# Code layout, output transfers and the order of the last sums in a decode kernel (attention over a KV cache, then a gated MLP)

**Chip, cores, metric.** One core of one Trainium2 chip. The metric is the device time of one execution in microseconds (us), the median of several executions on one chip. The record marks all runs told here as fast. Engines: PE is TensorE, DVE VectorE, ACT ScalarE, POOL GpSimd, SP SyncE. Times within an execution count from the start of its profiled span.

## The reference

For two sequences with one new token each, layer norm, 32 heads of attention over 8192 cached keys and values of 128 numbers, an output projection, then a second layer norm and a gated MLP, both with residuals:

```python
q = (x @ wq).reshape(B, Sq, Hq, Dh).transpose(0, 2, 1, 3)            # B=2, Sq=1, D=512, Hq=32, Dh=128
scores = einsum("bhqd,bhkd->bhqk", q, k_cache) * Dh ** -0.5           # k_cache, v_cache: (2, 32, 8192, 128) bf16
o = einsum("bhqk,bhkd->bhqd", softmax(scores), v_cache)
h = x + o.transpose(0, 2, 1, 3).reshape(B, Sq, Hq * Dh) @ wo
gate, up = layernorm(h) @ W_gate, layernorm(h) @ W_up                 # F = 1376
out = h + ((gate * (gate > 0)) * up) @ W_down
```

The two caches are 268 MB of the 281 MB that are read.

## The kernel before

All instructions are written to one list for each engine, with the semaphore waits worked out from what is read and written. Heads go in 16 steps of four; a step holds 8.39 MB of K and as much of V. DVE multiplies a K tile by the query in place and halves it to 8 columns; ACT takes the exponentials and their sums (`zm`); PE multiplies by V in a hardware loop; DVE picks the lanes. After the last step:

```python
s.op("pool", lambda: pool.tensor_tensor(out=zl, in0=zl, in1=zx, op=ALU.add),    # last exponential sums
     reads=["zm", "zx"], writes=["zm"], extra=[v_done(L)])
...                              # issue of gate, up0, up1, wda, wdb, wdc, wdd (the MLP's weights) on SP
s.op("pe", lambda: pe.matmul(out=zb, lhsT=same..., rhs=zm..., start=True, stop=True),
     reads=["zm", "same"], writes=["sm"])
lanes(L)
gather(B * NGR - 1)
s.op("dve", ... zs = zb * head_blk); red(zi, zs, ...); s.op("dve", ... zi = 1 / zi)
for k in range(NGR):
    s.op("dve", ... oc[k] = ou[:, :, k] * zi)
...                              # projection by wo, second layer norm, gate products
s.op("pe", lambda: y_rows(eye_of[:, 0:B], ar, first=True), ...)                 # residual into y
s.op("pe", lambda: mlp_in(1, up_ps, 0, KC - 1), reads=["hd", "up0"], writes=["mm1"])
s.op("pe", lambda: mlp_in(1, up_ps, KC - 1, KC), reads=["hd", "up1"], writes=["mm1"])
...                              # gate * up, its columns by PE, copied by ACT and DVE
for key, act_key, f0, f1 in (("wda", "act_t", 0, FT), ("wdb", "act_t", FT, FA),
                             ("wdc", "act_l", FA, FC - 1), ("wdd", "act_l", FC - 1, FC)):
    if key == "wdd":
        for eng in ("pe", "dve", "act"):
            s.cut(eng)                                                           # the late block begins
    s.op("pe", lambda f0=f0, f1=f1: add_y(f0, f1), reads=[act_key, key], writes=["y"])
y0, y1 = slice(0, B), slice(2 * Q, 2 * Q + B)          # partitions 0-1: left half of y, 64-65: right half
s.op("dve", lambda: dve.tensor_copy(y_row[y0], y_ps[y0]), reads=["y"], writes=["y0"])
s.op("act", lambda: act.activation(out=y_row[y1], in_=y_ps[y1], func=ACT.Copy), reads=["y"], writes=["y1"])
for b, eng, e in ((0, "sp", sync), (1, "act", act)):
    ends.append(s.dma(eng, f"dy{b}", lambda b=b, e=e: e.dma_start(
        out=out[b].rearrange("s (c n) -> (s c) n", n=D // 2),
        in_=y_row[b:P:2 * Q]), reads=["y0", "y1"]))    # partitions b and b + 64
```

Each of PE, ACT and DVE has its program in a main block, a late block with the end, and an unused block of `SPARE` empty instructions (15 for ACT, 1 for DVE, 7 for PE). At the start of the first two the program emits a branch hint for the branch at their end (BRANCH_PREFETCH_HINT in the trace: 0.04 to 0.06 us each, at 0.98 to 1.36 us and at 652.01 to 654.01 us).

The softmax here doesn't subtract the row's maximum and nothing guards it: scores larger than these inputs give would overflow.

Of the kernel before, what the change touches and what calls it, by code (L numbers as in the profile page):

```python
# [104 lines left out]
def kernel(  # L105
# [20 lines left out]
    G = 4  # L126
# [29 lines left out]
    RING = T * Dh  # L156
    SPARE = {"act": 15, "dve": 1, "pe": 7}

# [62 lines left out]
    s = Streams(nc, ("pe", "dve", "act", "pool", "sp"))  # L221
    for name in ("v_in", "v_two", "p_in", "p_two", "o_in", "half", "q0", "q1"):
        s.sem(name)
# [5 lines left out]
    for name, value in (("v_two", 16 * (NLOOP - 1)), ("p_two", NLOOP), ("o_in", 1), ("q0", 1),  # L229
                        ("q1", 1)):  # L230
        s.lists["pool"].append(((), lambda name=name, value=value: pool.sem_inc(s.sem(name), value),
                                None))
# [80 lines left out]
    def columns_of_x():  # L313
        for c in range(KC):
# [11 lines left out]
        reads=["xc", "st"], writes=["xd"])  # L326
    s.op("dve", lambda: dve.tensor_tensor(out=sq, in0=xd, in1=xd, op=ALU.mult), reads=["xd"],
         writes=["sq"])
# [5 lines left out]
    s.op("dve", lambda: dve.reciprocal(out=rstd, in_=rstd), reads=["rstd"], writes=["rstd"])  # L334
    s.op("dve", lambda: dve.tensor_tensor(
        out=xnb, in0=_view(xd, 0, [[B, KC], [1, B], [0, Q]]),
# [43 lines left out]

    def products(n, lo, hi, early=()):
        b, i = divmod(n, NQ)
        kp = kt[n % 2][:, lo:hi, :]
        keys = [f"k{n % 2}{x}" for x in parts(lo, hi)] or [f"k{n % 2}b", f"k{n % 2}c"]
        qk = [f"q{b}{i % 2}{h}" for h in range(G)]
        s.op("dve", lambda: dve.tensor_tensor(  # L386
            out=kp, in0=kp, in1=_view(qrep[:, b, i, :], 0, [[0, hi - lo], [1, Dh]]),
            op=ALU.mult), reads=keys + qk, writes=keys)
        width = Dh
        while width > 8:  # L390
            half = width // 2
            s.op("dve", lambda half=half, width=width: dve.tensor_tensor(  # L392
                out=kp[:, :, 0:half], in0=kp[:, :, 0:half], in1=kp[:, :, half:width], op=ALU.add),
                reads=keys + list(early), writes=keys)
            width = half
# [32 lines left out]
    def v_loop():  # L428
        base["pe"] = s.count["pe"]
        s.wait("pe", [s.last[k] for k in ("spread", "pm")])  # L430

        def take(name, value):
            pe.wait_ge(s.sem(name), value).then_inc(s.sem(name), -value)  # L433

        def fn():
            with pe.Fori(0, NGR * B):
                with pe.Fori(0, NS):
                    take("v_in", 16)
                    take("p_in", 1)
                    take("o_in", 1)  # L440
                    v_matmuls(0, T // 2).then_inc(s.sem("half"), 1)
                    take("v_two", 16)
                    v_matmuls(T // 2, LATE)
                    take("p_two", 1)
                    v_matmuls(LATE, T).then_inc(s.sem("pe"), 1)
                pe.wait_ge(s.sem("o_in"), 1)
                for u in range(NS):
                    last = pe.matmul(out=rep_ps[u * Q:(u + 1) * Q, :],  # L448
                                     lhsT=spread.rearrange("k h m -> k (h m)"), rhs=osb[:, u, :],
                                     start=True, stop=True, skip_group_check=True)  # L450
                last.then_inc(s.sem("pe"), 1)

        s.lists["pe"].append(((), fn, None))
        s.count["pe"] += NGR * B * (NS + 1)
# [24 lines left out]

    HALVES = (0, T // 2, T)  # L480
    load_v(0)
    v_loop()
    for n in range(N):
        b, i = divmod(n, NQ)
        z = zm[:, b, i:i + 1]
        for lo, hi in zip(HALVES[:-1], HALVES[1:]) if n == 0 else ((0, T if n < L else LATE),):
            products(n, lo, hi, [f"q{b}{i}{G - 1}" for b in range(B) for i in range(2)] if lo else ())
        if n:
            lanes(n - 1)
            s.last["pm"] = v_done(n - 1)  # L490
        if n % NS == 1 and n > 1:
# [21 lines left out]
    for k, lo, hi in WO:  # L513
# [17 lines left out]
    s.op("pool", lambda: pool.tensor_tensor(out=zl, in0=zl, in1=zx, op=ALU.add),  # L531
         reads=["zm", "zx"], writes=["zm"], extra=[v_done(L)])

# [16 lines left out]
    def load_down(key, f0, r0, rows, r):  # L550
# [9 lines left out]

    s.op("pe", lambda: pe.matmul(out=zb, lhsT=same.rearrange("p u h m -> p (u h m)"),
                                 rhs=zm.rearrange("p b i -> p (b i)"), start=True, stop=True),
         reads=["zm", "same"], writes=["sm"])
    lanes(L)
    gather(B * NGR - 1)
    s.op("dve", lambda: dve.tensor_tensor(
        out=zs, in0=zb.rearrange("p (g u) -> p g u", u=NS),
        in1=_view(head_blk, 0, [[0, B * NGR], [1, NS]]), op=ALU.mult), reads=["sm", "head"],
        writes=["zs"])
    red(zi, zs, AXIS.X, ["zs"], ["zi"])  # L570
    s.op("dve", lambda: dve.reciprocal(out=zi, in_=zi), reads=["zi"], writes=["zi"])
    for k in range(NGR):
        s.op("dve", lambda k=k: dve.tensor_tensor(
            out=oc[:, k * JG:(k + 1) * JG, :], in0=ou[:, :, k].rearrange("p b j -> p j b"),
            in1=_view(zi, k, [[0, JG], [NGR, B]]), op=ALU.mult),
            reads=[f"ou{b * NGR + k}" for b in range(B)] + ["zi"], writes=[f"oc{k}"])
# [65 lines left out]
    def mlp_in(g, ps, c0, c1):  # L642
        for c in range(c0, c1):
            for j in range(FT):
# [14 lines left out]
        out=gt, in0=gate_ps[:, 0:NM], scalar1=0.0, scalar2=r2, op0=ALU.max, op1=ALU.mult),  # L659
        reads=["gate_o", "r2"], writes=["osb0", "osb1", "osb2", "osb3"])  # L660
    s.op("pe", lambda: y_rows(eye_of[:, 0:B], ar, first=True), reads=["eye", "om"], writes=["y"])
    s.op("pe", lambda: mlp_in(1, up_ps, 0, KC - 1), reads=["hd", "up0"], writes=["mm1"])
    s.op("pe", lambda: mlp_in(1, up_ps, KC - 1, KC), reads=["hd", "up1"], writes=["mm1"])
    s.op("dve", lambda: dve.tensor_tensor(
        out=gn.rearrange("p (q j) -> p q j", j=FT), in0=_view(gt, 2 * P, [[1, NQR], [0, FT]]),
        in1=_view(head_blk, 0, [[0, NQR], [1, FT]]), op=ALU.mult),
        reads=["osb0", "head"], writes=["gn"])
    s.op("dve", lambda: dve.tensor_tensor(out=actr, in0=gt[:, 0:2 * P], in1=up_ps[:, 0:2 * P],
                                          op=ALU.mult), reads=["osb0", "mm1"], writes=["act"])
# [15 lines left out]
    def columns_of_rest():  # L685
        for u in range(3):
# [5 lines left out]
    s.op("pe", columns_of_act, reads=["act", "ident"], writes=["sm"])  # L692
    s.op("pe", columns_of_rest, reads=["act_n", "row_b"], writes=["rep"])
    s.op("act", lambda: act.activation(out=act_t[:, 0:FA], in_=act_ps, func=ACT.Copy),
         reads=["sm"], writes=["act_t"])
# [7 lines left out]
    for key, act_key, f0, f1 in (("wda", "act_t", 0, FT), ("wdb", "act_t", FT, FA),  # L703
                                 ("wdc", "act_l", FA, FC - 1), ("wdd", "act_l", FC - 1, FC)):
        if key == "wdd":
            for eng in ("pe", "dve", "act"):
                s.cut(eng)
        s.op("pe", lambda f0=f0, f1=f1: add_y(f0, f1), reads=[act_key, key], writes=["y"])
# [5 lines left out]
    ends = []  # L714
    for b, eng, e in ((0, "sp", sync), (1, "act", act)):
        ends.append(s.dma(eng, f"dy{b}", lambda b=b, e=e: e.dma_start(
            out=out[b].rearrange("s (c n) -> (s c) n", n=D // 2),
            in_=y_row[b:P:2 * Q]), reads=["y0", "y1"]))
    sems = [h.num for h in s.sems.values()]
# [8 lines left out]

    engines = (("sp", sync), ("pool", pool), ("act", act), ("dve", dve), ("pe", pe))
    inner = nc.cur_bb  # L730
    for name, engine in engines:
        only = OrderedEngineSet([engine.engine])
        if name in s.cuts:
            nc.br(f"{name}_all", engines=only)
        else:
            s.emit(name, engine)
            nc.br("done", engines=only)
    for name, engine in engines[2:]:
        only = OrderedEngineSet([engine.engine])
        nc.switch_body(f"{name}_all", parent=inner, valid_engines=only)  # L740
        top = nc.cur_bb
        turn = nc.alloc_registers(f"{name}_turn", engines=only)
        nc.regs_mov(turn, 0)
        loc = engine.mark_branch_hint_location()
        s.emit(name, engine, 0, s.cuts[name])
        engine.br_lt(turn, 9, on_true=f"{name}_late", on_false=f"{name}_spare").branch_hint(loc)
        nc.switch_body(f"{name}_late", parent=top, valid_engines=only)
        loc = engine.mark_branch_hint_location()
        s.emit(name, engine, s.cuts[name])
        engine.br_lt(turn, 9, on_true="done", on_false=f"{name}_spare").branch_hint(loc)  # L750
        nc.switch_body(f"{name}_spare", parent=top, valid_engines=only)
        for _ in range(SPARE[name]):
            engine.nop("spare")
        nc.br("done", engines=only)
    nc.switch_bb("done", parent=inner)
# [28 lines left out]
```

## Time and profile before

| | kernel before |
|---|---|
| time, median | 659.8 us (659.77 to 659.95, 3 runs) |
| span of the profiled run | 657.9 us |
| read from HBM | 281.06 MB |
| DVE busy | 613.6 us, 93% |
| DMA queue of the data (q1) busy | 99.0% |

The prediction below shows the slices, the queues and the chain. The DMA queues of the kernel before in the stretch from 640 to 646 us (packets, MB, share of the sixteen engines' time):

```profile
q1 hardware_dynamic: 292, 2.49, 99.4%
q8 instruction: 1, 0.02, 1.1%
```

One of 293 packets is no data but code (kind "instruction", 16384 bytes, 1.06 us at 642.40), brought in while the last weights are on their way. And the end of the instructions in order of time (start, duration, engine, line, operation, count, and in brackets what ended the idle time before):

```profile
654.42 0.38 ACT L712 ACTIVATE sc<-y 2x256 bf16<-2x256 f32 x1 [2.32 <-PE y L635]
654.42 0.41 DVE L711 CAST sc<-y 2x256 bf16<-2x256 f32 x1 [1.89 <-PE y L635]
654.88 0.62 SPq L716 DMA_DIRECT2D out_dram<-sc  x1
654.88 0.61 ACTq L716 DMA_DIRECT2D out_dram<-sc  x1
```

Both halves of the result are copied at once, and both output transfers take 0.6 us to issue, twice what SP needs for a K tile of 8.39 MB (0.33 us).

### The profile page before, as it was taken

The page shows a single profiled execution, that of the slowest core. Times are in us where ns is not written, and L with a number is a line of the kernel's source. Part 1 is how long each engine was busy: PE and PEld are TensorE (multiplying, and loading weights), DVE is VectorE, ACT ScalarE, POOL GpSimd, SP SyncE. Part 2 cuts the span into 40 slices and gives each one's busy share as a digit, 9 for nine tenths or more (in the row PEclk, how much of TensorE's full clock was granted, in tenths as well). Part 3 has the DMA queues.
Part 4 walks back from the last instruction along what each step waited for, and adds up shares of the span by engine and source line. Part 5 has one row for each costly group of instructions (what it writes and reads, how often), then busy time and mean ns, then how long its engine had stood idle before and what let it go on. Part 6 is the DMA issues. An engine that isn't in the chain of part 4 may idle for free.

```text
span 657.9 us, 3103 instructions
## 1 busy us (share of the span) xinstructions
PE 121.5 (18%) x1206; PEld 49.6 (8%) x1206; DVE 613.6 (93%) x177; ACT 61.9 (9%) x160; POOL 5.6 (1%) x25
## 2 busy tenths in 40 slices
PE   2400302003030110303012030300203030031256
PEld 1100101001010000101000010100101010010022
DVE  1699999999999999999999999999999999999963
ACT  2501001010101001010100101010010101001010
POOL 2000000000000000000000000000000000000000
PEclk9855755657555565755556575555657555565657
DMA  9999999999999999999999999999999999999996
GB/s 379 450 446 426 402 446 446 446 419 410 446 446 438 430 406 446 446 438 430 406 446 446 438 430 406 446 446 438 430 406 446 446 438 430 406 446 415 442 412 267
DMA packets 6614, 281.13 MB, mean 427 GB/s; under 512 B 744, under 2 KB 848, under 8 KB 1360
## 3 DMA queue, kind: packets, MB, share of 16 engines
q1 hardware_dynamic: 6596, 281.06, 99.0%
q8 instruction: 2, 0.03, 0.0%
q14 instruction: 4, 0.03, 0.0%
q10 hardware_dynamic: 12, 0.01, 0.0%
HBM read 281.06 MB, written 0.00 MB: 427 GB/s over the span
## 4 chain that ended last, share of the span: by engine, by line
DVE 75%; DMA 24%; issue 0%; SPq 0%; PE 0%
DVE k L386 34%; DVE k L392 33%; DMA k<-in_A_k_cache_dram 21%; DVE sc L243 4%; DMA k<-in_B_W_down_dram 3%; DVE osb L468 2%; DVE om L463 1%; SPq L539 0%; PE y L635 0%; DVE ou L243 0%; DVE rep L475 0%; SPq L551 0%; DVE sc L711 0%; SPq L294 0%; SPq L779 0%
## 5 line engine op out<-in xcount | busy, mean ns | idle before, releaser
L386 DVE TENSOR_TENSOR k<-k,qrep 128x32768 bf16<-128x32768 bf16 (+3 forms) x18 | 275.8, 15323 | 5.9 <-DMA k<-in_A_k_cache_dram 5.9
L392 DVE TENSOR_TENSOR k<-k 128x4096 bf16<-128x4096 bf16 (+6 forms) x72 | 267.4, 3714 | 2.5
L418 PE MATMUL o<-v,pm 128*32 128x512 bf16 x1024 | 96.3, 556 | 477.6 <-PEq L433 477.6
L405 ACT ACTIVATE pm<-sc 32x256 bf16<-32x256 f32 (+2 forms) x68 | 48.0, 706 | 560.3 <-DVE sc L243 559.6
L418 PEld LDWEIGHTS o<-v,pm 128*32 128x32 bf16 x1024 | 39.1, 132 | 534.3 <-issue 529.5
L243 DVE TENSOR_REDUCE sc<-k 128x256 f32<-128x2048 bf16 (+2 forms) x17 | 36.6, 2152 | 0.1
L468 DVE TENSOR_REDUCE osb<-om 128x128 f32<-128x512 f32 x16 | 16.3, 1018 | 0.6
L405 ACT ACTIVATION_READ_ACCUMULATOR pm<-sc 32x1 f32 x68 | 15.7, 232 | 0.0
L463 DVE TENSOR_TENSOR om<-o,turn_of 128x512 f32<-128x512 f32 x16 | 10.9, 683 | 3.7 <-PE o L418 3.7
L350 PE MATMUL mm<-v,om 128*64 x32 | 9.6, 436 | 7.1 <-PEq L348 7.0
L243 DVE TENSOR_REDUCE pick<-ident 128x8 f32<-128x128 bf16 x1 | 0.4, 381 | 10.9 <-ACT qrep L367 10.9
L367 ACT ACTIVATE qrep<-mm 32x512 bf16<-32x512 f32 x16 | 9.4, 587 | 6.7 <-PE mm L350 6.5
L448 PE MATMUL rep<-osb,spread 128*32 128x128 f32 x32 | 2.6, 421 | 37.9 <-DVE osb L468 37.9
L320 DVE COPY xc<-st 128x8 f32<-128x8 f32 x1 | 0.2, 167 | 6.0 <-PE st L315 6.0
L531 POOL TENSOR_TENSOR zm<-zm,zx 128x1 f32<-128x1 f32 x1 | 0.2, 190 | 626.5 <-PE o L418 626.5
L350 PEld LDWEIGHTS mm<-v,om 128*64 128x64 bf16 x32 | 3.9, 122 | 12.4 <-issue 11.6
L601 DVE STREAM_TRANSPOSE osb<-mm 128x512 f32<-128x512 f32 x1 | 0.7, 717 | 4.1 <-PE mm L587 4.1
L448 PEld LDWEIGHTS rep<-osb,spread 128*32 128x32 f32 x32 | 0.8, 142 | 40.3 <-DVE osb L468 40.3
L587 PE MATMUL mm<-k 128*2 128x512 bf16 x32 | 3.6, 624 | 0.0
L711 DVE CAST sc<-y 2x256 bf16<-2x256 f32 x1 | 0.4, 411 | 1.9 <-PE y L635 1.9
L475 DVE TENSOR_TENSOR rep<-rep,pick 128x128 f32<-128x128 f32 x4 | 1.2, 293 | 0.8 <-PE rep L448 0.8
L635 PE MATMUL y<-k 128*2 128x256 bf16 x22 | 1.8, 271 | 0.4 <-DMA k<-in_B_W_down_dram 0.3
(80 smaller groups left out, 32.2 us busy)
## 6 DMA issues: line engine op xcount, KB each, us to landing
v<-in_A_v_cache_dram SPq DMA_DIRECT2D x4, 4096.0 KB, 20.3
k<-in_A_k_cache_dram SPq DMA_DIRECT2D x2, 4096.0 KB, 26.1
v<-in_A_wq_dram SPq DMA_DIRECT2D x1, 4096.0 KB, 12.3
k<-in_A_wo_dram SPq DMA_DIRECT2D x1, 2048.0 KB, 20.2
k<-in_A_wo_dram SPq DMA_DIRECT2D x2, 1024.0 KB, 23.2
k<-in_B_W_gate_dram SPq DMA_DIRECT2D x1, 1376.0 KB, 13.7
k<-in_B_W_up_dram SPq DMA_DIRECT2D x1, 1032.0 KB, 15.8
k<-in_B_W_down_dram SPq DMA_DIRECT2D x2, 512.0 KB, 17.6
```

What stands on the lines that cost most here:

```text
L243: s.op("dve", lambda: dve.tensor_reduce(out=out_, in_=in_, axis=axis, op=ALU.add), reads=reads, writes=writes)
L350: last = pe.matmul(out=mm_ps[t][0:B * Q], lhsT=xnb[:, c].rearrange("p b q -> p (b q)"), rhs=wq_r[:, c, :, bass.ds(r * 2 + t, 1), :], start ...
L367: fn = lambda src=src, dst=dst: act.activation(out=dst, in_=src, func=ACT.Copy)
L386: s.op("dve", lambda: dve.tensor_tensor(out=kp, in0=kp, in1=_view(qrep[:, b, i, :], 0, [[0, hi - lo], [1, Dh]]), op=ALU.mult), reads=keys ...
L392: s.op("dve", lambda half=half, width=width: dve.tensor_tensor(out=kp[:, :, 0:half], in0=kp[:, :, 0:half], in1=kp[:, :, half:width], op=AL ...
L405: last = act.activation(out=p_of[ps, lo // TG:hi // TG, :, h], in_=sc2[n % 2][ps, lo:hi].rearrange("p (g t) -> p g t", t=TG), func=ACT.Exp ...
L418: last = pe.matmul(out=o_ps[g:g + W2], lhsT=pm[:, t // TG, :], rhs=vt[:, t:t + TG, :].rearrange("p t d -> p (t d)"), start=(t < P // Q * T ...
L448: last = pe.matmul(out=rep_ps[u * Q:(u + 1) * Q, :], lhsT=spread.rearrange("k h m -> k (h m)"), rhs=osb[:, u, :], start=True, stop=True, s ...
L463: s.op("dve", lambda: dve.tensor_tensor(out=om.rearrange("p (t d) -> p t d", d=Dh), in0=o_ps.rearrange("p (t d) -> p t d", d=Dh), in1=_vie ...
L468: s.op("dve", lambda: dve.tensor_reduce(out=osb[:, n % NS, :], in_=om.rearrange("p (t d) -> p d t", d=Dh), axis=AXIS.X, op=ALU.add), reads ...
L587: last = pe.matmul(out=ar_ps[g:g + B], lhsT=oc[:, k, :], rhs=wo_sb[:, k, :], start=False, stop=(k + P // Q >= NK), skip_group_check=True)
L635: end = pe.matmul(out=y_ps[c * 2 * Q:c * 2 * Q + m], lhsT=lhsT, rhs=rhs[:, c * D // 2:(c + 1) * D // 2], start=first, stop=last, skip_grou ...
```

## The change

Its intent: keep instruction fetches out of the time in which the last weights land, take work off the end, and let each output transfer wait for one copy only. The core of the diff (cut):

```diff
-    SPARE = {"act": 15, "dve": 1, "pe": 7}
+    MIDDLE = {"act": 30, "dve": 100, "pe": 9}
@@ first layer norm: two small operations from dve to pool
-    s.op("dve", lambda: dve.tensor_tensor(out=sq, in0=xd, in1=xd, op=ALU.mult), reads=["xd"],
+    s.op("pool", lambda: pool.tensor_tensor(out=sq, in0=xd, in1=xd, op=ALU.mult), reads=["xd"],
@@ V loop: the z product moves in, once for each group of four steps
+                take("z_in", 1)
+                pe.matmul(out=zb, lhsT=same..., rhs=zm..., start=True, stop=True).then_inc(s.sem("z_out"), 1)
@@ first tile: both halves halved once, the rest over the whole tile
+            products(n, 0, T // 2, to=Dh // 2)
+            products(n, T // 2, T, to=Dh // 2)
+            products(n, 0, T, Dh // 2, early=...)
@@ after the last step
     lanes(L)
-    gather(B * NGR - 1)
...
     for k in range(NGR):
+        if k == NGR - 1:
+            gather(B * NGR - 1)
@@ residual rows behind up, and the cut there
+    s.wait("pe", [s.last["up1"]])
     s.op("pe", lambda: mlp_in(1, up_ps, KC - 1, KC), reads=["hd", "up1"], writes=["mm1"])
+    s.cut("pe")
+    s.op("pe", lambda: y_rows(eye_of[:, 0:B], ar, first=True), reads=["eye", "om"], writes=["y"])
...
+    s.wait("dve", [up_mostly]); s.cut("dve")
...
+    s.wait("act", [s.last["up1"]]); s.cut("act")
@@ output
-    for b, eng, e in ((0, "sp", sync), (1, "act", act)):
-            out=out[b].rearrange("s (c n) -> (s c) n", n=D // 2),
-            in_=y_row[b:P:2 * Q]), reads=["y0", "y1"]))
+    for c, rows, eng, e in ((0, y0, "sp", sync), (1, y1, "act", act)):
+            out=out.rearrange("b s d -> (b s) d")[:, c * D // 2:(c + 1) * D // 2],
+            in_=y_row[rows]), reads=[f"y{c}"]))
@@ layout of pe, act and dve: gate, all, last, rest
+        block("gate"); fork(1, "last", False, "all")          # turn 0: on to "all"; turn 1: to "last"
+        block("all");  loc = engine.mark_branch_hint_location()
+        s.emit(name, engine, 0, MIDDLE[name]); fork(1, "rest", True, "last")
+        block("last"); s.emit(name, engine, s.cuts[name]);     fork(1, "done", False, "rest")
+        block("rest"); s.emit(name, engine, MIDDLE[name], s.cuts[name])
+        nc.regs_mov(turn, 1)
+        fork(9, "gate", True, "done").branch_hint(loc)         # back to the first block, then "last"
```

## The prediction

> **What bounds the kernel now.** I read the page first (busy shares, slices, queues), then the chain that ended last, then busy time by stretch, and the order of instructions over the last 25 us. DVE is busy 613.6 of 657.9 us, so it looks like the bound, but the slices say that it isn't alone:

> ```profile
> DVE  1699999999999999999999999999999999999963
> DMA  9999999999999999999999999999999999999996
> GB/s 379 450 446 426 402 446 446 446 419 410 446 446 438 430 406 446 446 438 430 406 446 446 438 430 406 446 446 438 430 406 446 446 438 430 406 446 415 442 412 267
> q1 hardware_dynamic: 6596, 281.06, 99.0%
> q8 instruction: 2, 0.03, 0.0%
> q14 instruction: 4, 0.03, 0.0%
> ```

> The DMA row is full from the first slice to the last but one. A KV step moves 2 x 8.39 MB, which at 446 GB/s is 37.6 us; a DVE step is 17.14 + 8.70 + 4.43 + 2.30 + 1.22 + 0.61 + 1.02 + 2.19 = 37.6 us from the chain. The two are level, and the chain decides:

> ```profile
> 22.94 8.70 DVE k L386
> ...
> 477.38 39.51 DMA k<-in_A_k_cache_dram
> 516.91 17.24 DVE k L386
> ...
> 555.32 38.98 DMA k<-in_A_k_cache_dram
> 594.32 12.97 DVE k L386
> ...
> 635.01 18.08 DMA k<-in_B_W_down_dram
> 653.09 0.04 issue
> 653.13 0.60 PE y L635 x8
> ...
> 654.42 0.41 DVE sc L711
> ```

> Up to 400 us the chain is all DVE; then it jumps three times onto a K load: DVE has caught up and waits for K. The end hangs on W_down. I also counted, from the DMA packet records of the trace, how many are in flight: 15 or 16 or more at every moment from 2.5 us to about 651.5 us (times from the span's start). The transfers form one unbroken run, and nothing before it can end earlier unless that run does. Busy time by stretch shows where it ends:

> ```profile
> 648.00:651.00 3.00, 3.00 (x30) 1.13 (x22) 1.42 (x4) 0.00 (x0) 0.00 (x0) 0.54 1.03 407
> 651.00:654.00 3.00, 1.89 (x27) 0.90 (x25) 1.02 (x3) 0.18 (x1) 0.00 (x0) 0.90 0.39 139
> ```

> The last two columns (DMA share, GB/s) fall from 1.03 to 0.39: the transfers run out in this stretch, but not together. In the packet records most of the sixteen engines finish their part of W_down between 651.6 and 652.5 us, one at 652.91 and one at 653.41 us. The laggards have a visible reason. Queue q8, kind "instruction", put one 16384-byte packet of 1.06 us on an engine at 642.40 us, when PE was at the start of the attention projection; q14 put two 8192-byte packets (0.33 and 0.31 us) in at 138.1 and 140.7 us. 653.41 - 1.06 = 652.35 and 652.91 - 0.63 = 652.28: the laggards are late by just these packets, since no engine has a pause in which to catch up. PE's last products sit right behind them:

> ```profile
> 649.45 1.69 PE L645 MATMUL mm<-k,sc 128*32 128x344 bf16 x16
> 653.13 0.31 PEld L635 LDWEIGHTS y<-k 128*2 128x2 bf16 x8 [0.56 <-DMA k<-in_B_W_down_dram]
> 654.10 0.09 PEld L635 LDWEIGHTS y<-k 128*2 128x2 bf16 x2 [0.19 <-DMA k<-in_B_W_down_dram]
> ```

> So the time is: the unbroken DMA run, plus the lag of its latest engine (about 0.9 us), plus 654.10 to 657.9 us for the last two products, two copies, the output and the closing barrier.

> [...]

> **The change part by part.**

> Start: two small operations of the layer norm go from DVE to POOL (0.17 and 0.42 us on DVE; perhaps 0.3 us slower by POOL with its waits, an estimate from the 0.2 to 0.3 us of its casts here). They end near 9.5 us, and the query projection waits for wq until 13.8 us. Worth 0.

> First tile: the two halves are halved once each, and the other three additions run over the whole tile. Before: 2 x (2.30 + 1.24 + 0.70) = 8.48 us; after: 4.43 + 2.30 + 1.22 = 7.95 us. With three gaps of 0.02, DVE gains 0.6 us at 57 us. DVE waits for K later (0.86 us at 594 us), so this only lengthens that wait. On the end: 0.

> z sums inside the V loop, gather behind: before, after the last lane sums (638.7 us) DVE did gather (0.30 + 0.29), zs 0.16, sum 0.17, reciprocal 0.18, product 0.15, and PE began its projection at 640.87 us. After, the z product runs while DVE does the lane sums, so zs to the first product (about 0.8 us with gaps) follow at once and PE starts near 639.6 us. Gain about 1.2 us there, if the output weights are down. The gate products started at 647.04 us, when gate landed anyway (its last packet ended at 646.43, and completions are seen some 0.5 us after). Alone worth 0; but it lets the weights, if they land 0.9 us sooner, be used sooner.

> Residual rows behind up: 0.5 us of PE moves from 648.92, where PE waited for up, to the wait for DVE's products (651.13 to 651.67). Neutral.

> Code layout: this is the part that can move the end. Each of PE, ACT and DVE gets a first block with the hint, a last part in the middle of the next block, and a rest behind it; after the rest it jumps back to the first block and on to the last part. [...]the packets at 642.4 and at 138 to 141 us go, or come only at the re-entry, after up has landed. Then the latest engine ends at about 652.5 (the next one in the list) instead of 653.41: -0.9 us for W_down and about -0.8 for gate and up. Also the branch and hint between the W_down parts (653.83 to 654.10 us on PE) go: -0.1, as they partly lie beside the landing. Against it: PE's, ACT's and DVE's two taken branches[...] (the ones here record 0.07 to 0.31 us), during waits for up, and a new ACT table load of 1.28 us. With up1 seen at about 649.5, ACT is through it at 651.2; its copy is due at 651.0. The W_down products need 1.3 us of PE, so they would be done at 652.8 if their data were there: still behind the landing. Costs 0.

> Output by tile: each output DMA waits for its own copy only; both copies end within 0.04 us (654.80, 654.83). -0.05 on ACT's issue at most.

> Sum: -0.9 - 0.1 - 0.05, of which I take back 0.25 because the fetches may return near the end on some engine: -0.8 us. 659.8 - 0.8 = 659.0 us.

> **Rivals.**

> (1) The re-entry misses: the block must be fetched at about 650.5 us, while the queues are full; a packet of 1.06 us plus about 1 us from issue to first packet (as SP's first load shows: issued 0.96, first packet 2.0) stalls PE, ACT or DVE by some 2 us. PE would be ready at 653.5 instead of 652.2 and end its products near 655: +0.6, 660.4 us.[...]

> (2) The fetches don't go but move: any fetch before the last W_down packet costs its engine the same 1 us. Then the landing stays and only 0.1 us is gained: 659.7 us.

> (3) DVE becomes the bound: no, DVE's work shrinks by 0.6 us and it already waits for K.

> (4) The exit gets quicker or slower beyond the span: three fetches start at 656.5 to 657.0 us, the longest ending at 657.8, as the span ends. The time is 1.9 us over the span, and if some of that is the exit's code, having it earlier may give another 0.5 us: 658.5.

> **Range and chances.** Two per cent is 13.2 us. The unbroken run of transfers is the same 281.06 MB and makes up 99% of the time, so no branch of the above gets near it; only an unforeseen repeated stall in the V loop could (sixteen steps of 1 us). I give that 0.01 and the other side 0.01. Within "same", the centre is 659.0, with (1) as the upper and (4) as the lower end: 658.1 to 660.3.

> **What would show it.** Right: no instruction packet between 140 and 648 us, all engines' last W_down packets within 0.6 us, the last W_down wait of PE ending near 653.2, span near 657.1. PE's projection starts near 639.6. The first tile's sum starts near 57.2 instead of 57.80, and DVE's waits for K grow by as much. Wrong: an idle time of PE, DVE or ACT of over 1 us ended by "issue" or its own sequencer after 650 us (rival 1), or a laggard engine as late as before (rival 2). A mean rate other than 446 GB/s in the middle slices would show that the chip, not the change, made the difference.

-0.9 (the last W_down packet near 652.5 instead of 653.41) - 0.1 (branch and hint) - 0.05 (output), and 0.25 taken back, is -0.8 us, so 659.0.

## The result

The changed kernel takes 658.12 us in the median of 4 runs (658.0 to 658.32), the kernel before beside it 659.88 us (659.77 to 660.26): 1.76 us less. The ratio is 0.9973, with a 95% interval of 0.9955 to 0.999. (A ratio here is the mean time of one kernel's fast runs over that of the other's of the same rounds, so not quite the ratio of the medians that are quoted.) "Within 2%" was right and the time fell just inside the range, but the gain was 1.76 us where 0.8 had been forecast, more than twice as much.

The page of the changed kernel: the slices and queues to set beside those in the prediction:

```profile
span 656.2 us, 3121 instructions
DMA  9999999999999999989999999989999999999997
GB/s 380 451 443 411 423 447 447 423 407 447 447 447 391 439 447 447 443 387 447 447 447 415 415 447 447 443 387 447 447 447 427 403 447 447 443 403 432 425 420 311
q1 hardware_dynamic: 6596, 281.06, 99.3%
q8 instruction: 2, 0.03, 0.0%
q14 instruction: 3, 0.02, 0.0%
```

The data moved (281.06 MB) and the rate of the full slices (447 GB/s, before 446) are as before. The chain that ended last has the same last links, but the weights land earlier:

```profile
594.05 12.97 DVE k L386
...
635.21 17.67 DMA k<-in_B_W_down_dram
652.88 0.14 issue
653.02 0.51 PE y L641 x6
653.53 0.02 issue
653.55 0.41 DVE sc L721
```

The copies start at 653.55 instead of 654.42 us: 0.87 of the 1.7 us by which the span is shorter. The DMA queues of the changed kernel say why; first from 640 to 646 us, where code came before:

```profile
q1 hardware_dynamic: 299, 2.55, 101.5%
```

then from 651 to 654 us:

```profile
q1 hardware_dynamic: 270, 0.38, 35.0%
q8 instruction: 1, 0.02, 3.4%
q14 instruction: 2, 0.02, 2.0%
```

All three code packets of this stretch came at 652.03 to 652.05 us (packet records), when the data was nearly through. The last W_down packet ended at 652.60 instead of 653.41 us, the last one of gate at 645.67 instead of 646.43.

The other half of the gain lies behind the copies. The order of instructions in the changed kernel:

```profile
639.35 0.58 PE L589 MATMUL mm<-k,ident 2*128 2x512 bf16 x1
642.89 1.02 PE L593 MATMUL mm<-k 128*2 128x512 bf16 x8 [0.30 <-DMA k<-in_A_wo_dram]
650.23 1.28 ACT L707 ACT_TABLE_LOAD   x1 [4.91 <-DMA k<-in_B_W_up_dram]
653.02 0.49 PE L641 MATMUL y<-k 128*2 128x256 bf16 x6 [0.15 <-DMA k<-in_B_W_down_dram]
653.55 0.41 DVE L721 CAST sc<-y 2x256 bf16<-2x256 f32 x1 [1.52 <-PE y L641]
653.96 0.27 ACTq L726 DMA_DIRECT2D out_dram<-sc  x1
653.99 0.31 SPq L726 DMA_DIRECT2D out_dram<-sc  x1
```

The issues take 0.27 and 0.31 us instead of 0.61 and 0.62. From the start of SP's issue to the first wait with which POOL learns of an output (a record of POOL's queue; it is ACT's) it is 653.99 to 655.09, 1.10 us; before it was 654.88 to 656.75, 1.88 us. The expectations below speak of this 0.78 us. But in the changed kernel this is not the later landing: POOL's next instruction waits for SP's output, and POOL has both at 655.26 instead of 656.81 us, so 1.27 instead of 1.93 us. The output is thus worth 0.66 us, which the prediction had put at 0.05. The packets agree: from SP's issue to the end of the last output packet it is 0.87 us, before 1.53 us.

The theory then (formed on the 0.78): two causes of about 0.8 us each, the fetches that no longer hold up one DMA engine before the last landing, and the output transfers. Rivals: (A) the output is not quicker by itself, but through what else ran then, or because it waits for one copy; (B) the earlier projection moved the end; and one side question, what in the output's form costs the time.

### The profile page after: what moved, and what is told of

The parts are those of the page before. It is cut to its first block, busy times and chain, and to the rows that moved or that the text cites. A ratio compares the mean times of both kernels' runs of the same rounds, so it can differ in the third digit from the quotient of the medians.

```text
span 656.2 us, 3121 instructions
## 1 busy us (share of the span) xinstructions
PE 120.3 (18%) x1212; PEld 49.8 (8%) x1212; DVE 612.7 (93%) x172; ACT 63.2 (10%) x161; POOL 6.4 (1%) x27
## 3 DMA queue, kind: packets, MB, share of 16 engines
q1 hardware_dynamic: 6596, 281.06, 99.3%
HBM read 281.06 MB, written 0.00 MB: 428 GB/s over the span
## 4 chain that ended last, share of the span: by engine, by line
DVE 75%; DMA 24%; issue 0%; SPq 0%; PE 0%
DVE k L386 34%; DVE k L391 33%; DMA k<-in_A_k_cache_dram 21%; DVE sc L243 4%; DMA k<-in_B_W_down_dram 3%; DVE osb L471 2%; DVE om L466 1%; SPq L547 0%; DVE ou L243 0%; SPq L559 0%; DVE rep L478 0%; PE y L641 0%; DVE sc L721 0%; SPq L294 0%; SPq L805 0%
## 5 line engine op out<-in xcount | busy, mean ns | idle before, releaser
L386 DVE TENSOR_TENSOR k<-k,qrep 128x32768 bf16<-128x32768 bf16 (+3 forms) x18 | 275.8, 15322 | 6.2 <-DMA k<-in_A_k_cache_dram 6.1
L391 DVE TENSOR_TENSOR k<-k 128x8192 bf16<-128x8192 bf16 (+4 forms) x69 | 266.9, 3868 | 2.4
L417 PE MATMUL o<-v,pm 128*32 128x512 bf16 x1024 | 93.8, 544 | 478.8 <-PEq L432 478.8
L446 PE MATMUL sm<-zm,same 128*128 128x16 f32 x8 | 1.8, 297 | 0.4 <-PEq L432 0.4
L240 POOL MEMSET pm<- 128x2048 bf16 x1 | 1.8, 1805 | 0.1
## 6 DMA issues: line engine op xcount, KB each, us to landing
k<-in_B_W_gate_dram SPq DMA_DIRECT2D x1, 1376.0 KB, 13.2
```

Of the source, the lines that this page charges most:

```text
L240: s.op("pool", lambda: pool.memset(pm, 0.0), writes=["pm"])
L386: s.op("dve", lambda: dve.tensor_tensor(out=kp, in0=kp, in1=_view(qrep[:, b, i, :], 0, [[0, hi - lo], [1, Dh]]), op=ALU.mult), reads=keys ...
L391: s.op("dve", lambda half=half, width=width: dve.tensor_tensor(out=kp[:, :, 0:half], in0=kp[:, :, 0:half], in1=kp[:, :, half:width], op=AL ...
L417: last = pe.matmul(out=o_ps[g:g + W2], lhsT=pm[:, t // TG, :], rhs=vt[:, t:t + TG, :].rearrange("p t d -> p (t d)"), start=(t < P // Q * T ...
```

## The experiments

Twelve runs, each beside the kernel before on the same chip (659.9 to 660.1 us). Times are medians.

| run | what it is | time, us | last W_down packet ends | output issues, us |
|---|---|---|---|---|
| (result) | the changed kernel | 658.12 | 652.60 | 0.27, 0.31 |
| e1 | before + output by tile | 661.49 | 653.71 | 0.27, 0.31 |
| e2 | changed, old output | 658.94 | 652.17 | 0.61, 0.62 |
| e3 | changed, old layout | 659.12 | 654.00 | 0.27, 0.31 |
| e4 | layout and output alone | 658.61 | 652.16 | 0.27, 0.31 |
| e9 | e1 + one spare instruction at the end | 660.93 | 653.54 | 0.27, 0.31 |
| e5 | changed, no hints | 659.47 | 653.52 | 0.26, 0.31 |
| e10 | the changed kernel again | 658.30 | 652.43 | 0.27, 0.31 |
| e11 | e4 again | 658.18 | 652.62 | 0.27, 0.31 |
| e12 | e1 + one instruction ahead of the end | 659.39 | 653.46 | 0.27, 0.31 |
| e6 | changed, outputs wait for both copies | 658.29 | 652.40 | 0.26, 0.31 |
| e7 | e6, source 64 partitions apart | 659.09 | 652.92 | 0.61, 0.61 |
| e8 | e6, target in one piece | 658.74 | 652.35 | 0.27, 0.31 |

The same code differs by up to 0.4 us (e4, e11), so differences below that are not read. The times on which the argument rests: e12 and e9 beside the kernel before, e5 and e11 beside e10, e7 and e8 beside e6. e2 and e3 were not run beside the changed kernel; their traces decide more than their times.

**e1: the output alone.** In the kernel before, only:

```diff
-    for b, eng, e in ((0, "sp", sync), (1, "act", act)):
-            out=out[b]..., in_=y_row[b:P:2 * Q]), reads=["y0", "y1"]))
+    for c, rows, eng, e in ((0, y0, "sp", sync), (1, y1, "act", act)):
+            out=out...[:, c * D // 2:(c + 1) * D // 2], in_=y_row[rows]), reads=[f"y{c}"]))
```

> The kernel before with the output by tile and nothing else. Theory (shape): the new kernel issued its two output DMAs in 0.27 and 0.31 us instead of 0.61 and 0.62, and from the start of the issue to POOL's last wait it took 1.10 us instead of 1.88; if the form of the transfer does that, this kernel has it too, ends about 0.75 us sooner than before (659.1), the instruction packet near 642 us and the last W_down packet near 653.4 us stay. Rival A (the recorded prediction): the output is worth 0.05 us, and the short issue came from the new code layout or from what else ran at that moment; then 659.8 and issues of 0.6 us.

Measured: 661.49 us (660.82 to 661.92), 1.6 us slower than before (ratio 1.002, interval 1.0006 to 1.0034). A miss, and the most instructive one. The output did become quicker: issues of 0.27 and 0.31 us, and 1.11 us from SP's issue to POOL's wait (655.14 to 656.25). But then ACT stood still. Its branch at the exit ran at 655.77 and its next instruction at 659.13 us, 3.3 us later, while the closing barrier waited for it; before, that gap was 0.5 us. So "the output by tile" is worth 0.66 us in the chain (POOL had both outputs 1.28 us after SP's issue, before 1.93) and cost 2.2 us elsewhere. Why is taken up in e9 and e12.

**e2: the changed kernel with the old output** (the diff of e1 turned round).

> The changed kernel with the output of before. Theory (shape): back to 0.6 us for each output issue, about 0.75 us later than the changed kernel: 658.9; last W_down packet still near 652.6. Rival A: 658.1 to 658.2, issues of 0.3 us.

Measured: 658.94 us (658.69 to 659.28), W_down's last packet at 652.17. The issues are 0.62 and 0.61 us again, in the new layout. This refutes rival A in its first form and gives the output 0.6 to 0.8 us, against e10 and the first result. In the traces, from SP's issue to the end of the span it is 2.88 us here and 2.23 us in the changed kernel: 0.65 us.

**e3: the changed kernel with the layout of before.**

```diff
-    (blocks gate, all, last, rest; cuts behind up; waits for up before them)
+    (blocks all, late, spare, as before; SPARE as before)
+        if key == "wdd":
+            for eng in ("pe", "dve", "act"):
+                s.cut(eng)
```

> The changed kernel with the code layout of before (late block before the last W_down product, unused spare block, old places of hints and no re-entry, no table load), all else as changed. Theory (fetch lag): the 16384-byte instruction packet is back near 640 to 643 us and the two of 8192 in the V loop, the last W_down packet ends near 653.4 instead of 652.6, and the time is about 0.8 us over the changed kernel: 658.9. Rival B (compute): the earlier projection (z sums, gather) made the end sooner; then the last W_down product still starts near 653.1 and the time is 658.1 to 658.3.

Measured: 659.12 us (659.0 to 659.76). The code packets are back inside the stream of data, at 172.7, 213.7 and 645.05 us. From 640 to 646 us its queues show:

```profile
q1 hardware_dynamic: 293, 2.50, 99.5%
q8 instruction: 1, 0.02, 1.1%
```

W_down ends at 654.00, 1.39 us later than in the changed kernel; of this 0.32 us is a later run of the data as a whole (its first packet of 4096 bytes started at 648.64 instead of 648.32), the rest is the lag. Rival B predicted no change here and fails.

**e4: layout and output alone** (z sums and gather, first tile, layer norm operations and residual rows as before).

> The changed kernel with only its code layout and its output: z sums and gather, first tile, layer norm operations and residual rows as before. Theory (fetch lag and output are all): 658.1 to 658.3, last W_down packet near 652.6. Rival B (compute): the projection starts 1.3 us later again and the products on gate and up with it, so that the end comes 0.5 to 1 us later, 658.6 to 659.1, with PE's W_down products no longer behind the landing.

Measured: 658.61 us (657.9 to 658.71), with the last W_down packet at 652.16. The profiled run, 657.9 us, is as short as any of the changed kernel; the median sits at the edge of what rival B asked for. Inconclusive alone, so it was repeated beside the changed kernel.

**e10 and e11: the changed kernel and e4 once more, side by side.**

> The changed kernel once more, to have it beside e11 on one chip. All theories: 658.0 to 658.7.

> The kernel of e4 (layout and output alone) once more beside the changed kernel on one chip. Theory (the compute parts are hidden): within 0.2 us of e10. Rival B (the earlier projection is worth something once W_down lands sooner): 0.3 to 0.6 us over e10, as the medians of two different calls suggest (658.61 against 658.12).

Measured: 658.30 us (658.04 to 658.75) and 658.18 us (658.11 to 658.49). The two overlap, and the smaller is the one without the compute parts. Rival B is out: z sums, gather, first tile, POOL operations and residual rows are together worth 0 within what these runs can tell.

**e5: no hints.**

```diff
-        loc = engine.mark_branch_hint_location()
...
-        fork(9, "gate", True, "done").branch_hint(loc)
+        fork(9, "gate", True, "done")
```

> The changed kernel without its branch hints. Theory[...]: without them the packets of 16384 and 8192 bytes are back near 642 us and in the V loop, so that W_down lands 0.8 us later, and [...]one or more of PE, ACT, DVE stands still for over 1 us after 649.5 us; 660 to 663. Rival: the hints do nothing and the order of the blocks alone puts the fetches at 652 us; then 658.1 to 658.6 and the same packets as in the changed kernel.

Measured: 659.47 us (659.33 to 659.6), 1.2 us over e10. Half of the theory held: without the hint the code packets are back, at 174.6, 213.1 and 644.59 us. The queues of this run from 640 to 646 us:

```profile
q1 hardware_dynamic: 293, 2.51, 100.2%
q8 instruction: 1, 0.02, 1.1%
```

W_down ends at 653.52 instead of 652.43 us. The other half failed: nobody stood still on the way back to the first block; each of the two branches of PE took 0.21 us, of ACT and DVE 0.04 to 0.07 us. What the hint changed in these runs is the time of the fetch (q8's packet at 652.03 us in the changed kernel, at 644.59 in e5); a stall that it saved did not show. It even has a price, which shows in the records of PE's branches: PE's last branch, at the end of its program, takes 0.20 us in e5 but 1.84 us in the changed kernel (653.12 to 654.96) and 1.40 to 1.94 us in all eight runs with the hints in the new layout, and it ends 1.32 to 1.39 us after the q8 code packet has. That PE stands there for its code is inferred from this. It shows no cost here, since POOL hears of both outputs later still (655.26 us). The span of e5 is 0.8 us longer than that of e10 (657.1, 656.3). The other 0.4 us lies outside the span: time minus span is 1.9 us in e10 (658.17 - 656.3) and 2.2 us in e5 (659.33 - 657.1). I do not know what runs there. One thing fits and no run tests it: where no code packet of the trace starts after the end of the span, the difference is 1.8 to 1.9 us (e3, e4, e11, e12); where one starts 1.2 us after that end it is 1.9 to 2.0 us (e10, e2), and in e5 one starts 1.7 us after it (658.77).

**e9: one more spare instruction at the end of ACT's program in e1.**

```diff
-    SPARE = {"act": 15, "dve": 1, "pe": 7}
+    SPARE = {"act": 16, "dve": 1, "pe": 7}
```

> The kernel before with the output by tile and one more unused instruction (16 instead of 15) at the end of ACT's program, which makes up for the one wait that the output by tile takes off ACT. Run e1 showed the output itself 0.78 us quicker but ACT standing still for 3.3 us between its exit branch and the next instruction. Theory (place of the exit code): [...]with the place restored ACT's gap is 0.5 us again and the time is about 659.1, 0.8 below before. Rival: ACT's stall comes with the new output itself (its transfer, or ACT's own semaphore); then 661 to 661.9 as in e1.

Measured: 660.93 us (660.81 to 661.71). A miss: ACT's gap at the exit is still 2.6 us (655.53 to 658.18). But the order of ACT's program shows why this was no fair test: the spare instructions lie behind the exit branches, and only what lies behind them moved back to its place. The exit branches themselves stayed one place too early.

**e12: one instruction ahead of ACT's end in e1.**

```diff
+    s.lists["act"].append(((), lambda: act.nop("place"), None))
     s.op("act", lambda: act.activation(out=y_row[y1], in_=y_ps[y1], func=ACT.Copy), reads=["y"],
```

> The kernel before with the output by tile and an instruction that does nothing at the start of ACT's last block, where the removed wait would have counted, so that everything behind it keeps its address. In e1 and e9 only one 8192-byte packet came near 138 us instead of two, and ACT stood still at its exit branch for 3.3 and 2.6 us; the spare instruction of e9 lay behind the exit branch. Theory (addresses): both packets (138 and 141 us) are back, ACT's gap at the exit is 0.5 us and the time is about 659.1. Rival (the output itself makes ACT wait): ACT's gap stays over 2 us, 660.8 to 661.7.

Measured: 659.39 us (659.11 to 659.46) against 660.05 of the kernel before: 0.66 us less. The gap of ACT at the exit is 0.47 us (655.50 to 655.98). The code packets from 130 to 150 us, first of e1:

```profile
q14 instruction: 1, 0.01, 0.1%
```

and of e12:

```profile
q14 instruction: 2, 0.02, 0.2%
```

In e1 one packet was missing. The wait that the output by tile took off ACT moved ACT's last branches by one place, and the early packet was lost. An instruction that does nothing, in the place of the wait, brings it back, and the stall goes (0.47 us against 3.3). Shown is that in this kernel one place more or less on ACT decides. That ACT stood waiting for the code which the missing packet would have brought is an inference: e1 has as many q14 packets as e12 in all (four; its last one starts at 660.0 us, behind the stall), but the last one before ACT goes on ends 1.8 us ahead of that in e1 and 1.05 us in e9, not a steady time as q8's packet does for PE (e5 above). Why the early packet did not come is not shown either.

**e6, e7, e8: what makes the output quick.** All in the changed kernel; both transfers wait for both copies.

```diff
 e6  reads=["y0", "y1"]                                              # shape as changed
 e7  reads=["y0", "y1"], in_=y_row[c:P:2 * Q]                        # source: partitions c and c + 64
 e8  reads=["y0", "y1"], out=out[c].rearrange("s (k n) -> (s k) n")  # target: one piece of 1 KB
```

> The changed kernel, where each output transfer waits for both copies, as before the change, but keeps its new shape. Theory (shape): issues of 0.27 and 0.31 us, time 658.1 to 658.4. Rival (the single wait makes it quicker): issues of 0.6 us and 658.9.

> The changed kernel with both waits, where each transfer reads two partitions 64 apart, as before the change, and writes two pieces of 512 bytes that lie 1 KB apart, as after it (the result is wrong on purpose). If the distance of the source partitions costs the time: issues of 0.6 us and about 658.9. If the shape of the target does: issues of 0.3 us and 658.1 to 658.4.

> The changed kernel with both waits, where each transfer reads two neighbouring partitions, as after the change, and writes one piece of 1 KB, as before it (the result is wrong on purpose). If the distance of the source partitions costs the time: issues of 0.3 us and 658.1 to 658.4. If the shape of the target does: issues of 0.6 us and about 658.9.

Measured: 658.29, 659.09 and 658.74 us; e7 and e8 give a wrong result. The issues in the order of instructions, e7 first:

```profile
654.35 0.61 SPq L726 DMA_DIRECT2D out_dram<-sc  x1
654.36 0.61 ACTq L726 DMA_DIRECT2D out_dram<-sc  x1
```

and e8:

```profile
653.98 0.31 SPq L726 DMA_DIRECT2D out_dram<-sc  x1
653.98 0.27 ACTq L726 DMA_DIRECT2D out_dram<-sc  x1
```

Between these runs it is the distance of the source partitions. Two partitions 64 apart cost 0.61 us of issue and 1.92 us from SP's issue until POOL has both outputs in e7 (654.35 to 656.27), two neighbours 0.3 and 1.36 us (e8: 653.98 to 655.34; e6: 653.99 to 655.36), whatever the target's shape. Only these two distances were tried. Two waits instead of one cost no issue time, and 0.09 us until POOL has both (1.36 in e6, 1.27 in the changed kernel). The spans of e7 and e6 differ by 0.92 us: 0.56 us is the distance, and 0.36 us is that e7's copies start later (653.90 instead of 653.54), as its W_down landed later. e8's median lies 0.45 us over e6, but its profiled run has the same span (656.3) and its four runs scatter from 658.15 to 659.17, so I read nothing from that.

## Why the prediction was wrong

The sum in the profiled runs: the copies start 0.87 us earlier (layout and branch), 0.02 us from copy to issue, the output 0.66 us, and 0.15 us that nobody forecast: from SP's issue to the end of the span the old layout takes longer with either output (3.05 and 2.88 us with the old output, 2.38 and 2.23 us with the new: before, e2, e12, changed). These make up the 1.70 us of the span; what in the old layout's exit takes the 0.15 us was not tested.

What stays open: why time minus span is 0.3 us larger without hints, the rule by which one instruction less on ACT cost the early fetch, and why a source 64 partitions apart is slower.

## What to carry to other kernels

When all DMA engines are busy to the end, ask what else goes through them: with a single code packet of 16384 bytes (1.06 us) inside the data, gate landed 0.77 us and W_down 0.81 us later than without it. A consumer waited for the last part of its load: before, PE's first product on up started at 649.45 us, about 0.05 us behind the last of that load's 16 semaphore updates (649.40) and 0.64 us behind the fifteenth (648.81). Moving the fetch to the end is no gift either: in the changed kernel PE then stood 1.84 us at its last branch, which only the output hid. Nothing hid the last transfer of this kernel, so read the duration of such an issue against others of the same engine, and try keeping its source partitions together (here 0.26 to 0.31 us of issue for neighbours, 0.61 to 0.62 us for two that are 64 apart). And in a kernel whose code blocks are placed by hand, one instruction more or less on an engine is itself a change: keep its place when you test a part alone, or a gain of 0.7 us shows as a loss of 1.6 us (e1).
